# Attention and gated feed-forward on one core: another order of the last stage's block products, later column sums, and w_out prepared at other times

## The chip, the cores and the metric

The kernel runs on one core of a Trainium2 chip. The metric is the device time of one execution in microseconds, lower is better. A core has five engines with queues of their own: TensorE (PE, with its weight loads as PEld), VectorE (DVE), ScalarE (ACT), GpSimd (POOL) and SyncE (SP), which here issues all DMAs. An engine executes its queue in order; an instruction that waits holds up all behind it.

## What is computed

```python
scores = where(causal mask, -1e9, (q @ k^T) / sqrt(64))      # q, k, v: 4 x 12 heads x 448 x 64
attn   = exp(scores - max); attn = attn / (sum(attn) + 1e-9)
x      = (attn @ v), heads side by side                      # 1792 tokens x 768
xn     = x / sqrt(mean(x * x) + 1e-6) * rms_g
g      = xn @ w_gate                                         # 768 x 1536
h      = g / (1 + exp(-g)) * (xn @ w_val)
out    = h @ w_out                                           # 1536 x 768
```

All of it is float32. A matmul operand is split into a rounded part h and the rest l (x = h + l), and a product is three matmuls: h·h, h·l and l·h.

## The kernel before

**Attention and FFN windows.** The tokens are cut into four groups (`GROUPS`) of 512, 512, 512 and 256 columns. Group 0's attention runs first. Then four FFN windows follow, window b for group b, and in each the attention steps of group b + 1 are laid between the FFN's matmuls. A window has 24 units; s counts them from 0 to 95. A unit is 18 matmuls for one 128-column piece of w_gate or w_val (`ffn_part`), in three ticks of six. `AT` says by which third of a unit a window's attention steps are done (of 72): 66, 62, 40. Window 2 (s = 48 to 71) has 30 steps to lay.

**The order is written out by hand.** The program emits instructions in the order of this loop, and each engine executes its own in that order. `post(n, fn)` emits fn n ticks later. `load_w(s + 6)` asks for the weights of a unit eleven ticks after unit s began, `split_w(s + 3)` splits them (ACT casts, POOL or DVE subtracts), and both use a ring of 4 buffers, `wr_p`. A unit's result is stored to `hd` in HBM.

**w_out** comes as 64-bit floats. `load_w64(s + 7)` and `convert(s + 5)` (L381 to L388) turn w_gate, w_val and then w_out's twelve pieces into float32 in HBM (`w32`), one piece per unit, w_out's at s = 19 to 30. Then `wo_sums` (L407 to L426), three times at `SUMS`, builds the sums of w_out's blocks that the last stage needs: loads, four additions 6 ticks later, four stores 12 ticks later. From the fifth unit after the last attention step on, `prep_load` and `prep_split` bring 15 of the 21 pieces of w_out's seven block operands into SBUF and split them (L480, L482), one per unit, in the ring `wr_p`. The last six come at the start of the last stage.

**rms** (L327 to L342) runs once per group. Two matmuls with `ones` sum the squares over the features into bank t; ACT takes the root, DVE four reciprocals. Then four small matmuls put the same sums into columns, again in bank t, and root and reciprocal follow at once. `rcol` scales the rows of the output.

**The last stage** multiplies h by w_out with Strassen-Winograd products: per pair of 128-token blocks seven products (`product`, 18 matmuls of 384 columns, 49 in all for 7 pairs). Products 0 and 1 add up in one PSUM bank, products 5 and 6 in another. `operand(q + 4)`, four products ahead, makes the next stationary operand (ACT cast L512, POOL subtraction L99; for i = 2 four DVE additions first, L504 to L507). `result` takes the sum out of the bank, combines it and stores a block of the output. `load_h` brings a pair's h (1.5 MB) from HBM. PSUM has eight banks: a, t, x, y, m twice, s twice.

Of the kernel before, what the change touches and what calls it, by code (L numbers as in the profile page):

```python
# [14 lines left out]
ALU = mybir.AluOpType  # L15
# [35 lines left out]
HALF = DM // 2  # L51
WARM = [9, 0, 0, 2]
EXTRA = 4
AT = [66, 62, 40, 1]
DP = 3
SUMS = (34, 39, 44)


@with_exitstack
def attention_ffn(ctx: ExitStack, tc: tile.TileContext, qk0, qk1, qk2, v, v2, w, g, out):  # L60
# [19 lines left out]
    ht_p = pool("ht", 6, ffn, side="left")  # L80
    xx_p = pool("xx", 1, ffn, side="left")
    xr_stack = ctx.enter_context(ExitStack())
    xr_p = pool("xr", 6, xr_stack, side="left")
    raw = pool("raw", 4, att, side="right")
    sp_p = pool("sp", 6, att, side="right")
# [226 lines left out]
    def split_x(at):  # L312
        if not waiting:
            return
        b, c = waiting[0]
        if b and c >= 3 and at < (b * NU - 1) * 3 + c // 2:
            return
        waiting.pop(0)
        x, gc = xr[b, c][:, : cols(b)], g_sb[:, c: c + 1]
        h, l = (xx_p.tile([P, W], F32R, tag=f"{n}{c}", name=n, bufs=1 + (c < 3))[:, : cols(b)]  # L320
                for n in ("xh", "xl"))
        nc.scalar.mul(h, x, gc)
        post((T["xl0"] if c < NP - 1 else T["xl"]) if b == 0 else int(c < 3), lambda: nc.vector.scalar_tensor_tensor(  # L323
            out=l, in0=x, scalar=gc, in1=f32(h), op0=ALU.mult, op1=ALU.subtract))
        xh[b, c], xl[b, c] = h, l

    def rms(b, sq):  # L327

        ps = bank("t")[:, : cols(b)]
        nc.tensor.matmul(ps, ones, sq, start=True, stop=True)  # L330
        r = rinv[b] = xx_p.tile([P, W], F32, tag="rms", name="rms", bufs=2)[:, : cols(b)]
        nc.scalar.activation(r, ps, AF.Sqrt, bias=eps, scale=1.0 / DM)
        for i in range(cols(b) // P):
            sl = slice(i * P, (i + 1) * P)
            nc.vector.reciprocal(r[:, sl], r[:, sl])
        n = cols(b) // P
        ps = bank("t")[:, :n]
        for i in range(n):
            nc.tensor.matmul(ps[:, i: i + 1], sq[:, i * P: (i + 1) * P], ones[:, :1], start=True, stop=True)
        rc = rcol[:, W // P * b: W // P * b + n]  # L340
        nc.scalar.activation(rc, ps, AF.Sqrt, bias=eps4, scale=4.0 / DM)
        nc.vector.reciprocal(rc, rc)  # L342

# [86 lines left out]
    def ffn_part(s, ks):  # L432
# [22 lines left out]
        else:  # L455
# [3 lines left out]
                out=hd[b][:, :, f, :], in_=t.rearrange("p (n t) -> p n t", t=2 * P)))  # L459


    ORDER = (("a11", 0), ("a12", 0), ("s2", 0), ("s1", 0), ("s4", 0), ("s3", 0), ("a22", 0))
    WSRC = [lambda m: wo_tile(m, 0), lambda m: wo_tile(m, 1), lambda m: wsum[1][m], lambda m: wsum[0][m],
            lambda m: wo_tile(m + 3, 1), lambda m: wsum[2][m], lambda m: wsum[3][m]]
    wc, side = {}, {}

    def prep_load(j):

        i, m = divmod(j, 3)
        t = wr_p.tile([P, DM], F32, tag="w", name="w_o")  # L470
        nc.sync.dma_start(out=t, in_=WSRC[i](m))
        wt["o", j] = t

# [20 lines left out]
    def operand(q):  # L494

        if q >= 7 * NPAIR:
            return
        p, i = divmod(q, 7)
        t = hp[p]
        a11, a12, a21, a22 = (t[:, 6 * k: 6 * k + 6, P * e: P * e + P] for e in (0, 1) for k in (0, 1))  # L500
        if i == 2:
            s1, s2 = (side["r"].tile([P, 6, P], F32, tag=n, name=n) for n in ("s1", "s2"))
            op["s1"] = s1
            nc.vector.tensor_tensor(s1, a21, a22, op=ALU.add)  # L504
            nc.vector.tensor_tensor(s2, s1, a11, op=ALU.subtract)  # L505
            nc.vector.tensor_tensor(a21, a11, a21, op=ALU.subtract)
            nc.vector.tensor_tensor(a12, a12, s2, op=ALU.subtract)  # L507
            src = s2
        else:
            src = (a11, a12, None, op.get("s1"), a12, a21, a22)[i]  # L510
        h, l = (side["o", q % 4].tile([P, 6, P], F32R, tag=n, name=n) for n in ("oh", "ol"))
        nc.scalar.copy(h, src)  # L512
        pool_op(l, src, ALU.subtract, f32(h))
        op[q] = h, l

    def product(q):
        p, i = divmod(q, 7)
        if i != 1 and i != 6:
            op["ps"] = bank("msssxyy"[i] if i not in (2, 3) else "s", 2 if i in (0, 2, 3) else 1)[:, :HALF]
        ps = op["ps"]  # L520
        (ah, al), (bh, bl) = op.pop(q), wc[i]
        again = i in (1, 6)
        for k in range(6):
            for n, (x, y) in enumerate(((ah, bh), (ah, bl), (al, bh))):
                nc.tensor.matmul(ps, x[:, k, :], y[:, k], start=(k + n == 0 and not again),  # L525
                                 stop=(k == 5 and n == 2), skip_group_check=again)
        return ps

    def result(q, ps):


        p, i = divmod(q, 7)
        r = side["r"]

        def tmp(n):
            op[n] = r.tile([P, HALF], F32, tag=n, name=n)
            return op[n]

        def store(c, e, n):
            nc.sync.dma_start(out=out[P * (2 * p + e): P * (2 * p + e + 1), HALF * n: HALF * (n + 1)], in_=c)  # L540

        def res(u, e, n):
            c = r.tile([P, HALF], F32, tag="c", name="c", bufs=4)
            if u is None:
                nc.scalar.mul(c, ps, rcol[:, 2 * p + e: 2 * p + e + 1])
            else:
                nc.vector.tensor_tensor(c, u, ps, op=ALU.add)  # L547
                nc.scalar.mul(c, c, rcol[:, 2 * p + e: 2 * p + e + 1])  # L548
            store(c, e, n)

        if i == 0:
            nc.scalar.copy(tmp("m1"), ps)  # L552
        elif i == 1:
            res(None, 0, 0)
        elif i == 2:
            u = tmp("u2")
            nc.vector.tensor_tensor(u, op["m1"], ps, op=ALU.add)
        elif i == 3:
            u = tmp("u4")
            nc.vector.tensor_tensor(u, op["u2"], ps, op=ALU.add)  # L560
        elif i == 4:
            res(op["u4"], 0, 1)
        elif i == 5:
            res(op["u4"], 1, 1)
        else:
            res(op["u2"], 1, 0)

# [46 lines left out]
    with tc.manual_schedule():  # L614
# [57 lines left out]
        for s in range(NG * NU):  # L672
            w_ = s // NU
            if s % NU == 0:
                at, goal = done, ends[w_ + 1] + 2 * (w_ == 0) if w_ + 1 < NG else done
            post(T["ld"], lambda s=s: load_w64(s + 7))
            post(T["ld1"], lambda s=s: load_w(s + 6))
            if s in SUMS:
                wo_sums(SUMS.index(s))
            for k0 in (0, 2, 4):  # L680
                ks = [k for k in (k0, k0 + 1) if (s, k) not in early]
                if ks:
                    ffn_part(s, ks)
                i = 3 * (s % NU) + k0 // 2 + 1
                while done < goal and (done - at) < (goal - at) * i / AT[w_]:
                    steps[done]()
                    done += 1
                for _ in range(2):
                    split_x(3 * s + k0 // 2)
                if k0 == 0:  # L690
                    convert(s + 5)
                if k0 == (0 if s < 3 else 4):
                    split_w(s + 3)
                for fn in prep.pop(now[0], []):
                    fn()
                tick()
            if done == len(steps) and att_end is None:
                att_end = s
            if att_end is not None and s == att_end + 5:
                att.close()  # L700
                side["w"] = pool("wc", 1, side="right", reuse_waits="tile")
                for i in range(5):
                    side["w", i] = side["w"]
            if att_end is not None and s >= att_end + 5 and preps < 15:
                prep_load(preps)
                post(2, lambda j=preps: prep_split(j))
                preps += 1
            if s == (NG - 1) * NU + 6:
                assert not waiting
                xr_stack.close()  # L710
                side["h", 0] = side["o", 0] = pool("h0", 1, side="right", reuse_waits="tile")
                load_h(0)
            if s == NG * NU - 4:
                operand(0)
        assert not prep and preps == 15
        while later:
            tick()
        ffn.close()
        side["r"] = side["h", 1] = side["w", 5] = side["w", 6] = pool("r", 1, side="left", reuse_waits="tile")
        ring = pool("ring", 3, side="left", reuse_waits="tile")  # L720
        for i in (1, 2, 3):
            side["o", i] = ring
        operand(1)
        operand(2)
        for j in (15, 16, 17):
            prep_load(j)
        load_h(1)
        operand(3)
        for q in range(7 * NPAIR):
# [6 lines left out]
                        prep_load(j)  # L736
            if q and q % 7 == 0:
                load_h(q // 7 + 1)
            operand(q + 4)
            result(q, ps_)  # L740
            tick()


# [45 lines left out]
```

## Time and profile before

| | us |
|---|---|
| median of 3 runs | 807.07 (806.69 to 812.16) |
| the profiled execution | 806.67 |
| its span, first to last instruction | 804.7 |
| PE busy in the span | 712.0 (88%) |
| DVE, ACT, POOL busy | 448.8, 379.1, 431.8 |

A row of a stage view gives, for a stretch of the span, its length and each engine's busy time with the number of instructions, then the granted TensorE clock (PEclk, 1.00 is 2.4 GHz), the DMA engines' share and GB/s. A row of waits gives who stood idle for whom: us in total, how often, and the longest. A matmul's busy time overlaps the next one's, so the pace is read from starts.

### The profile page before, as it was taken

The page shows a single profiled execution, that of the slowest core. Times are in us where ns is not written, and L with a number is a line of the kernel's source. Part 1 is how long each engine was busy: PE and PEld are TensorE (multiplying, and loading weights), DVE is VectorE, ACT ScalarE, POOL GpSimd, SP SyncE. Part 2 cuts the span into 40 slices and gives each one's busy share as a digit, 9 for nine tenths or more (in the row PEclk, how much of TensorE's full clock was granted, in tenths as well). Part 3 has the DMA queues.
Part 4 walks back from the last instruction along what each step waited for, and adds up shares of the span by engine and source line. Part 5 has one row for each costly group of instructions (what it writes and reads, how often), then busy time and mean ns, then how long its engine had stood idle before and what let it go on. Part 6 is the DMA issues. An engine that isn't in the chain of part 4 may idle for free. (4 is left out here: it accounts for less than half of the span.)

```text
span 804.7 us, 12298 instructions
## 1 busy us (share of the span) xinstructions
PE 712.0 (88%) x4302; PEld 583.7 (73%) x4302; DVE 448.8 (56%) x893; ACT 379.1 (47%) x824; POOL 431.8 (54%) x343
## 2 busy tenths in 40 slices
PE   8788799997978999997999989985968888978977
PEld 6555567775756777766778778875967877978977
DVE  5866768887789956573756432475564133033131
ACT  7867778685454544443535132454443223222321
POOL 5985344485338668553653634554458345445441
PEclk9998899999899999998999999998989889989989
DMA  8653858787587685875857414688642312321201
GB/s 271 224 180 112 268 192 265 257 278 277 189 301 253 243 289 203 307 272 180 271 175 208 146 60 150 210 264 267 209 164 73 108 38 89 109 82 56 99 30 39
DMA packets 61708, 149.04 MB, mean 185 GB/s; under 512 B 7056, under 2 KB 27536, under 8 KB 60752
## 3 DMA queue, kind: packets, MB, share of 16 engines
q1 hardware_dynamic: 61648, 148.27, 55.1%
q8 instruction: 34, 0.56, 0.3%
q14 instruction: 26, 0.21, 0.1%
HBM read 112.86 MB, written 35.39 MB: 184 GB/s over the span
## 5 line engine op out<-in xcount | busy, mean ns | idle before, releaser
L442 PE MATMUL m_ps<-xh,w_h 128*128 128x512 f32 (+1 forms) x570 | 225.2, 395 | 7.1 <-DVE gr L450 6.5
L444 PE MATMUL m_ps<-xh,w_l 128*128 128x512 f32 (+1 forms) x570 | 212.9, 374 | 5.5 <-POOL w_l L99 5.5
L443 PE MATMUL m_ps<-xl,w_h 128*128 128x512 f32 (+1 forms) x570 | 212.0, 372 | 0.1
L99 POOL TENSOR_TENSOR w_l<-w_r,w_h 128x768 fp32r<-128x768 f32 x60 | 112.8, 1890 | 62.4 <-ACT w_h L396 61.5
L207 POOL TENSOR_SCALAR sp<-sp,rs 128x384 f32<-128x384 f32 (+3 forms) x132 | 86.5, 672 | 91.1 <-DVE rs L211 89.8
L442 PEld LDWEIGHTS m_ps<-xh,w_h 128*128 128x128 f32 x570 | 111.4, 195 | 25.9 <-ACT woh L480 6.8
L444 PEld LDWEIGHTS m_ps<-xh,w_l 128*128 128x128 f32 x570 | 110.8, 194 | 25.6 <-POOL w_l L99 6.7
L443 PEld LDWEIGHTS m_ps<-xl,w_h 128*128 128x128 f32 x570 | 111.4, 195 | 13.6 <-DVE xl L323 0.4
L202 ACT ACTIVATE sp<-sp,nm 128x128 f32<-128x128 f32 (+3 forms) x168 | 87.1, 521 | 60.4 <-DVE nm L199 60.4
L99 POOL TENSOR_TENSOR ol<-h_r,oh 128x768 fp32r<-128x768 f32 x35 | 68.9, 1971 | 53.3 <-ACT oh L512 53.3
L451 ACT ACTIVATE t_sb<-gr 128x512 f32<-128x512 f32 (+1 forms) x48 | 27.7, 577 | 130.4 <-DVE gr L450 130.4
L273 PEld LDWEIGHTS a_ps<-pt,v_r 128*64 128x64 f32 (+1 forms) x864 | 40.8, 138 | 44.7 <-ACT pt L253 13.4
L273 PE MATMUL a_ps<-pt,v_r 128*64 128x128 f32 (+2 forms) x864 | 58.5, 269 | 16.5 <-ACT pt L253 8.0
L396 ACT CAST w_h<-w_r 128x768 fp32r<-128x768 f32 x72 | 58.7, 825 | 23.9 <-DMA w_r<-w 20.0
L382 POOL TENSOR_SCALAR w<-w 128x768 f32<-128x768 f32 x36 | 44.3, 1230 | 38.6 <-ACT w_c L381 27.6
L512 ACT CAST oh<-h_r 128x768 fp32r<-128x768 f32 x35 | 29.2, 835 | 72.1 <-PE m_ps L525 31.2
L199 DVE CUSTOM_DVE_ANT_0 sp<-s_ps,mask 128x128 f32<-128x128 f32 (+3 forms) x136 | 49.8, 414 | 19.5 <-PE s_ps L190 17.9
L247 PE MATMUL t_ps<-ident,sp 128*128 128x128 f32 (+1 forms) x309 | 51.8, 280 | 7.3 <-DVE pt L251 6.0
L251 DVE COPY pt<-t_ps 128x384 f32<-128x384 f32 (+1 forms) x71 | 42.3, 596 | 27.4 <-PE t_ps L247 27.4
L247 PEld LDWEIGHTS t_ps<-ident,sp 128*128 128x128 f32 (+1 forms) x309 | 38.2, 140 | 23.3 <-DVE pt L251 6.0
L99 POOL TENSOR_TENSOR ol<-s,oh 128x768 fp32r<-128x768 f32 x14 | 30.4, 2177 | 45.7 <-ACT oh L512 45.7
L525 PE MATMUL y_ps<-woh,oh 128*128 128x384 f32 x84 | 34.4, 410 | 23.0 <-DVE c L547 23.0
(112 smaller groups left out, 1335.8 us busy)
## 6 DMA issues: line engine op xcount, KB each, us to landing
w<-in_w SPq DMA_DIRECT2D x36, 768.0 KB, 5.7
w_r<-w SPq DMA_DIRECT2D x72, 384.0 KB, 4.4
qk_r<-in_qk SPq DMA_DIRECT2D x48, 256.0 KB, 4.3
h_r<-hd SPq DMA_DIRECT2D x7, 1536.0 KB, 6.7
w<-w_c SPq DMA_DIRECT2D x24, 384.0 KB, 2.8
hd<-t_sb SPq DMA_DIRECT2D x36, 256.0 KB, 3.8
qk_r<-in_qk SPq DMA_DIRECT2D x12, 512.0 KB, 4.4
v_r<-in_v SPq DMA_DIRECT2D x12, 448.0 KB, 8.2
```

The source lines that it names most:

```text
L99: nc.gpsimd.tensor_tensor(out_, a, b, op=op)
L199: nc.vector.tensor_tensor_reduce(out=sp, in0=ps, in1=mk, scale=nsc, scalar=3.0e38, op0=ALU.add, op1=ALU.min, accum_out=nm)
L202: post(T["exp" if p >= ENDS[0] else "exp0"], lambda: nc.scalar.activation(sp, sp, AF.Exp, bias=nm, scale=-1.0, accum_out=sm))
L207: pr["norms"].append(lambda: nc.gpsimd.tensor_scalar(sp, sp, rs, 1.0, op0=ALU.mult, op1=ALU.mult))
L247: nc.tensor.transpose(ps[:kb, at: at + P], pr["sp"][e][:, o + kb * j: o + kb * (j + 1)], ident)
L251: nc.vector.tensor_copy(pt[:kb, :at], ps[:kb, :at])
L273: nc.tensor.matmul(av_ps[e * D: (e + 1) * D, p % 2, q0: q0 + n], raw_v[p][:kb, h, j, e, :], pr["pt", e][:kb, a0: a0 + n], start=(j == 0), ...
L382: (T["c1"], lambda: nc.gpsimd.tensor_scalar(hf_, hf_, 0.0, 1.0, op0=ALU.mult, op1=ALU.mult)),
L396: nc.scalar.copy(h, t)
L442: nc.tensor.matmul(ps, wh[:, k, :], mh, start=(first and k == ks[0]), stop=False)
L443: nc.tensor.matmul(ps, wh[:, k, :], ml, start=False, stop=False)
L444: nc.tensor.matmul(ps, wl[:, k, :], mh, start=False, stop=(last and k == 5))
```

## The change

In the last stage the seven products of a pair run in another order. Before, their banks were m m s s x y y, where the second m and the second y add to the bank of the product just before. After, they are m s m s y x y. The operands, w_out's pieces (`WSRC`) and the results follow that order; the additions of the long operand stand at i = 1 (three of them) and i = 5 (the fourth). `result(q)` is emitted ahead of `operand(q + 4)`. Operand 1 is made before the stage begins, with s1, s2 and the first operands' buffers in the pool h0; operands have two pools of 2 buffers each, and `c` has 3 in place of 4.

In `rms` the small matmuls move 8 ticks later and into bank x, and DVE copies their sums; one root and one reciprocal for all groups stand at the head of the last stage, ahead of `load_h(1)` and operand 3.

w_out's pieces are loaded from s = 22 and converted from s = 26 on, one per two units. `wo_sums` runs at s = 50, 54 and 58. Window 1 lays its attention steps up to third 64 and window 2 up to third 54. From the second unit after the last attention step, two pieces per unit are loaded and split, out of a pool of 2 buffers of their own. The first three chunks of x's parts for even groups come from a pool `xa`, which is given back earlier.

```diff
-AT = [66, 62, 40, 1]
+AT = [66, 64, 54, 1]
-SUMS = (34, 39, 44)
+SUMS = (50, 54, 58)
+LATE = 22
...
@@ rms
-        n = cols(b) // P
-        ps = bank("t")[:, :n]
-        for i in range(n):
-            nc.tensor.matmul(ps[:, i: i + 1], sq[:, i * P: (i + 1) * P], ones[:, :1], start=True, stop=True)
-        rc = rcol[:, W // P * b: W // P * b + n]
-        nc.scalar.activation(rc, ps, AF.Sqrt, bias=eps4, scale=4.0 / DM)
-        nc.vector.reciprocal(rc, rc)
+
+        def columns():
+            n = cols(b) // P
+            ps = bank("x")[:, :n]
+            for i in range(n):
+                nc.tensor.matmul(ps[:, i: i + 1], sq[:, i * P: (i + 1) * P], ones[:, :1], start=True, stop=True)
+            rc = rcol[:, W // P * b: W // P * b + n]
+            nc.vector.tensor_copy(rc, ps)
+
+        post(8, columns)
...
@@ prep_load
-        t = wr_p.tile([P, DM], F32, tag="w", name="w_o")
+        t = side["w"].tile([P, DM], F32, tag="w", name="w_o", bufs=2) if j < 15 else \
+            wr_p.tile([P, DM], F32, tag="w", name="w_o")
...
@@ operand
-        if i == 2:
-            s1, s2 = (side["r"].tile([P, 6, P], F32, tag=n, name=n) for n in ("s1", "s2"))
-            op["s1"] = s1
+        if i == 1:
+            s1, s2 = (side["s"].tile([P, 6, P], F32, tag=n, name=n) for n in ("s1", "s2"))
+            op["s1"], op["s2"] = s1, s2
             nc.vector.tensor_tensor(s1, a21, a22, op=ALU.add)
             nc.vector.tensor_tensor(s2, s1, a11, op=ALU.subtract)
             nc.vector.tensor_tensor(a21, a11, a21, op=ALU.subtract)
-            nc.vector.tensor_tensor(a12, a12, s2, op=ALU.subtract)
-            src = s2
-        else:
-            src = (a11, a12, None, op.get("s1"), a12, a21, a22)[i]
-        h, l = (side["o", q % 4].tile([P, 6, P], F32R, tag=n, name=n) for n in ("oh", "ol"))
+        if i == 5:
+            nc.vector.tensor_tensor(a12, a12, op["s2"], op=ALU.subtract)
+        src = (a11, op.get("s2"), a12, op.get("s1"), a21, a12, a22)[i]
+        h, l = (side["o", q % 4].tile([P, 6, P], F32R, tag=n, name=n, bufs=2) for n in ("oh", "ol"))
...
@@ product
-        if i != 1 and i != 6:
-            op["ps"] = bank("msssxyy"[i] if i not in (2, 3) else "s", 2 if i in (0, 2, 3) else 1)[:, :HALF]
-        ps = op["ps"]
+        n = "msmsyxy"[i]
+        if i not in (2, 6):
+            op["bank", n] = bank(n, 2 if n in "ms" else 1)[:, :HALF]
+        ps = op["bank", n]
...
@@ the loop over units
-            post(T["ld"], lambda s=s: load_w64(s + 7))
+            c = s + 7 if s + 7 < NU else NU + (s - LATE) // 2 if s >= LATE and (s - LATE) % 2 == 0 else NC
+            post(T["ld"], lambda c=c: load_w64(c))
...
-                    convert(s + 5)
+                    convert(s + 5 if s + 5 < NU else NU + (s - LATE - 4) // 2
+                            if s >= LATE + 4 and (s - LATE) % 2 == 0 else NC)
...
-            if att_end is not None and s >= att_end + 5 and preps < 15:
-                prep_load(preps)
-                post(2, lambda j=preps: prep_split(j))
-                preps += 1
+            if att_end is not None and s >= att_end + 2:
+                for j in range(preps, min(preps + 2, 15)):
+                    prep_load(j)
+                    post(2, lambda j=j: prep_split(j))
+                    preps += 1
...
             if s == NG * NU - 4:
                 operand(0)
+            if s == NG * NU - 2:
+                operand(1)
...
@@ the last stage
-        operand(1)
         operand(2)
         for j in (15, 16, 17):
             prep_load(j)
+        nc.scalar.activation(rcol, rcol, AF.Sqrt, bias=eps4, scale=4.0 / DM)
+        nc.vector.reciprocal(rcol, rcol)
         load_h(1)
         operand(3)
         for q in range(7 * NPAIR):
...
+            result(q, ps_)
             operand(q + 4)
-            result(q, ps_)
             tick()
```

## Rows read from the trace of the kernel before

**Rows 1.** Stages: length; PE, PEld, DVE, ACT, POOL busy; PEclk; DMA; GB/s.
```profile
420.00:480.00 60.00, 57.84 (x517) 45.38 (x516) 28.03 (x64) 23.13 (x49) 26.64 (x24) 0.99 0.46 141
480.00:593.10 113.10, 100.45 (x618) 90.74 (x617) 54.05 (x73) 46.94 (x69) 54.17 (x29) 0.96 0.60 198
593.10:804.70 211.60, 171.62 (x885) 167.02 (x883) 63.44 (x67) 61.90 (x89) 102.79 (x51) 0.90 0.23 83
```
**Rows 2.** The chain that ended last: start us, us, what.
```profile
630.92 3.02 PE m_ps L525 x17
...
638.70 6.25 PE s_ps L525 x36
...
649.56 2.48 DVE s L505
...
653.77 0.48 DVE c L547
654.39 5.96 PE y_ps L525 x18
660.35 2.98 PE m_ps L525 x17
...
797.25 3.42 PE y_ps L525 x18
```
**Rows 3.** Timeline of the last stage's start: start us, us, instruction, [idle before <-releaser].
```profile
593.23 0.33 PE L525 MATMUL m_ps<-woh,oh 128*128 128x384 f32 x1
...
601.85 0.47 ACT L552 COPY m<-m_ps 128x384 f32<-128x384 f32 x1
...
605.53 0.83 ACT L480 CAST woh<-w_o 128x768 fp32r<-128x768 f32 x1 [3.22 <-DMA w_o<-wsum]
```
**Rows 4.** Waits of TensorE over the run: us in total, times, longest.
```profile
PE y_ps L525 <- DVE c L547: 23.0, 7, 6.4
PE m_ps L525 <- ACT m L552: 12.9, 7, 5.8
PE t_ps L339 <- ACT rms L332: 11.2, 4, 4.6
...
PE m_ps L442 <- DVE gr L450: 6.5, 2, 5.3
PE t_ps L247 <- DVE pt L251: 6.0, 5, 3.2
PE m_ps L444 <- POOL w_l L99: 5.5, 5, 1.6
```
**Rows 5.** Stages again, around one pause of the last stage.
```profile
629.32:653.21 23.89, 20.75 (x117) 20.10 (x116) 6.74 (x8) 7.74 (x11) 11.68 (x7) 1.00 0.25 91
653.21:660.04 6.83, 5.65 (x18) 5.68 (x19) 1.03 (x2) 0.61 (x1) 2.25 (x1) 0.50 0.08 29
683.93:687.34 3.41, 3.41 (x12) 3.41 (x12) 0.00 (x0) 0.35 (x1) 0.91 (x1) 0.50 0.16 58
```
**Rows 6.** Groups of instructions from 602 on: busy us, mean ns; idle before.
```profile
L99 POOL TENSOR_TENSOR ol<-h_r,oh 128x768 fp32r<-128x768 f32 x33 | 65.2, 1979 | 47.7 <-ACT oh L512 47.7
...
L512 ACT CAST oh<-h_r 128x768 fp32r<-128x768 f32 x32 | 26.7, 835 | 69.7 <-PE m_ps L525 31.2 <-PE s_ps L525 24.7 <-PE x_ps L525 13.8
```
**Rows 7.** DMA issues on the page: count, KB each, median us to landing.
```profile
h_r<-hd SPq DMA_DIRECT2D x7, 1536.0 KB, 6.7
```
**Rows 8.** Stages again, behind the second `rms`.
```profile
199.24:206.07 6.83, 6.42 (x21) 5.45 (x22) 6.44 (x8) 1.34 (x3) 1.82 (x1) 0.50 0.00 1
```
**Rows 9.** Splits and units: w_o landing, POOL's split, `gr` per two units.
```profile
DMA to landing us min/median/max: 3.2/3.9/8.7
...
L99 POOL TENSOR_TENSOR wol<-w_o,woh 128x768 fp32r<-128x768 f32 x8 | 16.2, 2027 | 18.9 <-ACT woh L480 18.9
...
L450 DVE TENSOR_TENSOR gr<-m_ps,rms x5: 690/692/692, 486.8 to 519.5; 128x512 f32<-128x512 f32 x5
...
L450 DVE TENSOR_TENSOR gr<-m_ps,rms x7: 409/424/425, 562.7 to 589.4; 128x256 f32<-128x256 f32 x7
```

More of the change, by code (lines that the diff above doesn't have):

```diff
@@ L82, in attention_ffn @@
     xr_stack = ctx.enter_context(ExitStack())
+    xa_p = pool("xa", 1, xr_stack, side="left")
     xr_p = pool("xr", 6, xr_stack, side="left")
@@ L319, in split_x @@
         x, gc = xr[b, c][:, : cols(b)], g_sb[:, c: c + 1]
-        h, l = (xx_p.tile([P, W], F32R, tag=f"{n}{c}", name=n, bufs=1 + (c < 3))[:, : cols(b)]
+        h, l = ((xa_p if c < 3 and b % 2 == 0 else xx_p).tile([P, W], F32R, tag=f"{n}{c}", name=n)[:, : cols(b)]
                 for n in ("xh", "xl"))
@@ L459, in ffn_part @@
                 out=hd[b][:, :, f, :], in_=t.rearrange("p (n t) -> p n t", t=2 * P)))
-    ORDER = (("a11", 0), ("a12", 0), ("s2", 0), ("s1", 0), ("s4", 0), ("s3", 0), ("a22", 0))
-    WSRC = [lambda m: wo_tile(m, 0), lambda m: wo_tile(m, 1), lambda m: wsum[1][m], lambda m: wsum[0][m],
-            lambda m: wo_tile(m + 3, 1), lambda m: wsum[2][m], lambda m: wsum[3][m]]
+    WSRC = [lambda m: wo_tile(m, 0), lambda m: wsum[1][m], lambda m: wo_tile(m, 1), lambda m: wsum[0][m],
+            lambda m: wsum[2][m], lambda m: wo_tile(m + 3, 1), lambda m: wsum[3][m]]
     wc, side = {}, {}
@@ L517, in product @@
         p, i = divmod(q, 7)
-        if i != 1 and i != 6:
-            op["ps"] = bank("msssxyy"[i] if i not in (2, 3) else "s", 2 if i in (0, 2, 3) else 1)[:, :HALF]
-        ps = op["ps"]
+        n = "msmsyxy"[i]
+        if i not in (2, 6):
+            op["bank", n] = bank(n, 2 if n in "ms" else 1)[:, :HALF]
+        ps = op["bank", n]
         (ah, al), (bh, bl) = op.pop(q), wc[i]
-        again = i in (1, 6)
+        again = i in (2, 6)
         for k in range(6):
@@ L542, in res @@
         def res(u, e, n):
-            c = r.tile([P, HALF], F32, tag="c", name="c", bufs=4)
+            c = r.tile([P, HALF], F32, tag="c", name="c", bufs=3)
             if u is None:
@@ L553, in result @@
         elif i == 1:
+            nc.vector.tensor_tensor(tmp("u2"), op["m1"], ps, op=ALU.add)
+        elif i == 2:
             res(None, 0, 0)
-        elif i == 2:
-            u = tmp("u2")
-            nc.vector.tensor_tensor(u, op["m1"], ps, op=ALU.add)
         elif i == 3:
-            u = tmp("u4")
-            nc.vector.tensor_tensor(u, op["u2"], ps, op=ALU.add)
+            nc.vector.tensor_tensor(tmp("u4"), op["u2"], ps, op=ALU.add)
         elif i == 4:
+            res(op["u4"], 1, 1)
+        elif i == 5:
             res(op["u4"], 0, 1)
-        elif i == 5:
-            res(op["u4"], 1, 1)
         else:
@@ L698, in attention_ffn @@
                 att_end = s
-            if att_end is not None and s == att_end + 5:
+            if att_end is not None and s == att_end + 2:
                 att.close()
@@ L710, in attention_ffn @@
                 xr_stack.close()
-                side["h", 0] = side["o", 0] = pool("h0", 1, side="right", reuse_waits="tile")
+                side["h", 0] = side["o", 0] = side["o", 1] = side["s"] = pool("h0", 1, side="right", reuse_waits="tile")
                 load_h(0)
@@ L719, in attention_ffn @@
         side["r"] = side["h", 1] = side["w", 5] = side["w", 6] = pool("r", 1, side="left", reuse_waits="tile")
-        ring = pool("ring", 3, side="left", reuse_waits="tile")
-        for i in (1, 2, 3):
+        ring = pool("ring", 2, side="left", reuse_waits="tile")
+        for i in (2, 3):
             side["o", i] = ring
-        operand(1)
         operand(2)
```

## Prediction

> **What bounds the kernel now.** I read the stages first [rows 1]. In the last one, 593.1 to 804.7 us, no other engine is busy for half of the time, TensorE is, and its granted clock is only 0.90. So TensorE there is both waiting and slow. The chain of waits says why [rows 2]. Two products in a row take 6.25 us for 36 matmuls, 3.13 us each. From the first product (593.23 [rows 3]) to the end of the last (797.25 + 3.42 = 800.67) the 49 products take 207.4 us; 49 × 3.13 is 153.4. So 54.0 us of this stage is not work. It has three causes.
>
> First, inside a pair (about 29.4 us, 630.92 to 660.35, against 7 × 3.13 = 21.9) the second y product must wait until VectorE has read the first one's sum, and VectorE does that read (653.77) after four additions of `operand`. The second m product likewise waits for ScalarE's copy, which stands behind a cast. Over the run these waits are 23.0 and 12.9 us [rows 4]. Second, each such pause is followed by a stretch at half clock [rows 5]: 1.00 (2.4 GHz) for 23.9 us up to the pause, then 0.50, the 1.2 GHz level, for 6.83 us; the y product in it takes 5.96 us instead of 3.13 [rows 2]. Third, the first pair takes 37.7 us (593.23 to 630.92).
>
> Before 593 the waits of TensorE [rows 4] name three smaller places: 11.2 us in `rms` (L339, for the square root that reads bank t), 6.0 us of transposes behind VectorE, and 6.5 + 5.5 us of FFN matmuls behind the weight splits.
>
> **The last stage.** The order of banks becomes m s m s y x y. A product that adds to a bank now has another product, 3.13 us, between it and its predecessor. What must fit under it: for m, the copy (0.47 us [rows 3]) behind no cast of the same step, since `result` now comes before `operand`; for y, one addition of 0.5 us [rows 2]. Both fit, so I cost the 23.0 + 12.9 us as gone apart from the first pair.
>
> Is something else late next? `operand(q + 4)` is issued after product q, so it has three products, 9.4 us, before it is needed. A plain operand needs a cast of 0.83 and a POOL subtraction of 1.98 [rows 6], 2.8 us. The long one (i = 1) needs s1 and s2, at 2.48 each as s2 has it now [rows 2], behind one addition of 0.5, then cast and subtraction: 8.3 us. It fits, by 1.1 us. Per pair POOL needs 7 × 1.98 = 13.9 us of 21.9 and VectorE less. h_r is asked for at the head of a pair, lands 6.7 us later [rows 7] and is used after four products, 12.5 us. `c` with 3 buffers: a buffer comes back after at least 12 us of products, while one store is 192 KB. So six of the seven pairs at 21.9: 131.4 us.
>
> First pair. Operands 0 and 1 now stand ready before the stage. But the three casts of w_out pieces (j = 15 to 17) still stand ahead of the copy of m on ScalarE; that copy came at 601.85, 8.6 us after the start [rows 3]. The product that needs it is now the third, due 6.3 us after the start, so some 2.8 us of pause (9.1 before), and half a clock stretch, 1.7 to 3.4 us. The next three casts come after their loads (605.53 and later [rows 3]) and hold up the casts of operands 5 and 6 by some 3 us. The sum is 8 us over 21.9; bounds 2 (all hidden) and 15.8 (as now). Stage: 131.4 + 21.9 + 8 = 161.3, a gain of 46.1 us (38 to 52).
>
> Do the many changes of bank cost clock? Four products in a row in four banks (s, s, x, y, from 638.70 on [rows 2]) ran without a wait inside the stretch at 1.00 [rows 5]. The Trainium skill, page "TensorE: Matmul & The Clock Gate", section "A second HAM failure mode: psum-queue depth-cycling", tells of a kernel that cycled through PSUM banks at each iteration and whose clock kept switching between its levels. By the row the stage gains 46.1 us, by that rule some 18 less (rival A). I take the row; no such switching without a pause shows in this trace.
>
> **Column sums.** `rms` no longer waits for the root before the small matmuls: they go to bank x, 8 ticks later. Of 11.2 us [rows 4] the first of the four cases stays, since transposes into t follow it at once; in the second a transpose follows after six matmuls, so a little may stay: gain 9. The pause was followed by half clock ([rows 8] is one of three such stretches, 6.83, 6.83 and 3.41 us long; half of each is lost, 8.5 together). I take 6 of it. Unknown: the wait for bank x; the nearest row, VectorE's read of a bank at 0.5 us [rows 2], bounds it at 2 us over the four. Net 15 (8 to 20). The four roots become one at the head of the last stage; its table load sits in front of operand 3's cast, within the 8 us above.
>
> **Conversions of w_out.** Twelve of them move from one per unit (s = 19 to 30) to one per two units (26 to 48). Each is VectorE work, two shifts, and in that part of the run VectorE is what the transposes waited for: most of the 6.0 us [rows 4]. I take 4 (0 to 8, with a half-clock stretch that follows one of them). The same work lands where TensorE hardly waits now. The sums move to s = 50, 54, 58, four units apart: their store (12 ticks) now falls just ahead of the next sums' loads into the same tiles, so SP stands until it has landed, with q, k, v and weight loads behind it. Weight loads run about three units ahead, so I charge 2 us (0 to 8). Spreading attention (AT 54 instead of 40) moves matmuls between units; I cost that at nothing: TensorE is busy for 57.8 of 60 us there as it is (420 to 480 [rows 1]).
>
> **Splits of w_out.** The last attention step moves from s = 60 to 65 (30·i/54 > 29 gives i = 53). So 15 pieces go two per unit over s = 67 to 74, from a pool of their own with 2 buffers. Each load must wait until the piece two before has been split: landing 3.9 and POOL 2.03 [rows 9] with a cast of 0.83 [rows 6] make 6.8 us per unit. A unit takes 4.1 us in the third window (486.8 to 519.5 over 8 units) and 2.2 in the fourth [rows 9]. SP holds these loads in line with the FFN's weight loads, so the weights become late: 7 × 6.8 = 47.6 us of loads against 4 × 4.1 + 3 × 2.2 = 23.0 of matmuls, less some 8 us of lead (three units of 4.1 less a landing of 3.9), a stall of 17, and 4 behind h_r (6.7 [rows 7] less a unit of 2.2): 21 us. Before, one piece per unit ran to s = 79 in a pool shared with the weights, and cost 6.5 + 5.5 us of waits [rows 4] and some 3.4 of clock (0.96 over 113 us [rows 1] is 4.5, a part of it from the stretch before): 15.4. Loss 5; bounds +12 (weights with four buffers of their own never wait) and -18 (each stall with a half-clock stretch).
>
> **Sum.** 46 + 15 + 4 - 2 - 5 = 58. The span of 804.7 becomes 746.7; the profiled execution took 806.67, 1.97 more, so 748.6; it lies 0.4 under the median of the runs, 807.07. I say 748.5.
>
> **Rivals.**
> A. The clock does not hold in the last stage: every pair keeps the half-clock stretches of now (6.83 and 3.41 us in turn [rows 5], 2.6 us lost a pair), with no wait left. For it: each pair now has one. Against: each follows a pause of over a microsecond that the change takes out. 7 × 2.6 = 18 us: 767. It is the rule of the Trainium skill cited above (page "TensorE: Matmul & The Clock Gate", same section). Chance 0.07.
> B. The split pool is worse than costed: ScalarE stands at a cast whose load is late, tanh and weight casts behind it, and TensorE drops to half clock between. The bound of -18 and 8 us lost at the sums: 768. For it: the 6.8 against 2.2 us. Against: the same chain ran before with half the pieces per unit. Chance 0.10.
> C. The reordering does not free the products: the long operand's chain, at 8.3 us plus queueing, is late once per pair by 2 us with a clock stretch of 1.7 to 3.4 behind it. 7 × 4.5 = 31: 780. Against: the POOL subtraction before it is done 3 us earlier, so VectorE runs s1 and s2 alone. Chance 0.06.
> D. Slower. At the splits the gain of 58 is lost if an iteration costs (58 + 17 + 23 + 8) / 7 = 15.1 us instead of 6.8, as each 1 us more costs 7. The longest landing seen there, 8.7 [rows 9], in every iteration gives 11.6, or 782; from 15.1 on it decides, and at 16.3 the time is 815. Chance 0.02.
> E. Better: the splits gain 6 instead of losing 5, the first pair costs 4 instead of 8, the conversions give 8, and all clock after `rms` comes back: 748.5 - 11 - 4 - 4 - 2.5 = 727. Chance 0.12.
> The forecast itself, 735 to 762, has 0.63.
>
> **Range.** It leaves out D, C and the far halves of E and B, 0.19 in all: 730 to 769. Faster by over 1% (about what a measurement of this kernel can tell from no change) holds all cases but D and the far end of C: 0.94; same 0.04; slower 0.02.
>
> **What would show it.** Right: in the last stage pairs of 21.9 us, granted clock near 1.00 after the first pair, no wait of y for `c` or of m for `m` beyond the first pair; L339 without a wait on the root; the transposes' wait on VectorE shorter. Splits: loads of w_o in twos, 6 to 7 us apart, and FFN units of 5 to 7 us at s = 72 to 77. Wrong: pairs over 23 us with a wait on `ol` or `oh` (C), half clock without a pause (A), or SP standing at `w_o` for over 8 us a time (B, D).

## The result

After: 748.74 us (median of 4 runs, 746.04 to 750.16) against 807.10 before (4 runs, 806.69 to 812.16): a ratio of 0.926, 95% interval 0.921 to 0.931. The profiled execution took 747.44 us, its span is 745.6.

The stage view of after (columns as in [rows 1]; the last stage begins at 578.4):

```profile
480.00:578.40 98.40, 83.86 (x533) 77.91 (x532) 47.16 (x69) 41.75 (x61) 44.13 (x24) 0.90 0.62 206
578.40:745.60 167.20, 157.76 (x884) 156.51 (x883) 51.90 (x67) 63.65 (x91) 96.23 (x51) 0.98 0.29 105
...
502.30:550.70 48.40, 35.43 (x217) 33.48 (x216) 23.34 (x33) 21.89 (x34) 20.52 (x12) 0.79 0.72 240
...
602.90:609.80 6.90, 6.05 (x19) 6.05 (x20) 2.54 (x3) 1.42 (x3) 6.87 (x4) 0.51 0.08 29
609.80:741.20 131.40, 131.40 (x754) 131.40 (x753) 34.40 (x51) 47.56 (x69) 71.70 (x39) 1.00 0.27 97
```

From 609.8 on TensorE is busy all of the time at clock 1.00; before, this stage stood at 0.90. What is left of trouble lies in two places: the units s = 72 to 84 (502.3 to 550.7, clock 0.79) and the first pair, with its one stretch at half clock from 602.9. The chain that ended last, against [rows 2]:

```profile
609.24 3.46 PE m_ps L530 x18
612.70 3.14 PE s_ps L530 x18
...
622.09 3.12 PE y_ps L530 x18
625.21 3.18 PE x_ps L530 x18
628.39 3.18 PE y_ps L530 x18
631.57 3.18 PE m_ps L530 x18
...
738.40 3.19 PE y_ps L530 x18
```

From 609.24 on every product follows the last without a gap, the second y (628.39) too. TensorE's waits over the run, against [rows 4]:

```profile
PE m_ps L447 <- DVE gr L455: 5.7, 2, 3.6
PE x_ps L249 <- DVE rcol L345: 4.2, 1, 4.2
...
PE t_ps L249 <- DVE pt L253: 3.4, 4, 1.6
PE x_ps L343 <- DVE nm L201: 3.3, 1, 3.3
PE m_ps L449 <- POOL w_l L101: 3.0, 4, 1.6
...
PE m_ps L530 <- ACT m L557: 2.4, 1, 2.4
PE y_ps L530 <- POOL ol L101: 2.0, 1, 2.0
...
PE y_ps L530 <- POOL wol L101: 1.0, 1, 1.0
PE t_ps L249 <- ACT rms L334: 1.0, 2, 0.8
```

The 23.0 us of y behind `c` are gone, of the 12.9 of m 2.4 are left, of the 11.2 in `rms` 1.0. New are two waits around the column sums in bank x, 4.2 and 3.3; the first of them, as r9 below shows, stands where another wait stood before.

Where the time went, stage by stage, in the profiled executions. A column is one kernel, a row the time from the first matmul of unit s to that of the next unit named, in us; r3, r14, r5, r6 and r13 are runs below.

| | before | r3 | r14 | after | r5 | r6 | r13 |
|---|---|---|---|---|---|---|---|
| s = 3 to 24 | 127.5 | 123.0 | 118.4 | 118.6 | 124.7 | 118.3 | 118.7 |
| 24 to 48 | 175.0 | 174.0 | 165.3 | 159.8 | 169.8 | 159.4 | 159.1 |
| 48 to 72 | 133.5 | 133.3 | 132.4 | 137.5 | 131.5 | 137.5 | 135.3 |
| 72 to 84 | 42.1 | 42.8 | 41.5 | 48.4 | 48.0 | 41.2 | 38.0 |
| 84 to the first product | 27.7 | 27.8 | 28.1 | 27.8 | 27.7 | 27.7 | 28.0 |
| last stage | 207.4 | 204.0 | 206.6 | 163.1 | 160.1 | 160.5 | 157.0 |

Of the 59 us, 44.3 come from the last stage, 24.1 from the first two windows, and 10.3 are lost between s = 48 and 84.

### The profile page after: what moved, and what is told of

Its sections match the earlier page's. It is cut to its first block, busy times and chain, and to the rows that moved or that the text cites. A ratio compares the mean times of both kernels' runs of the same rounds, so it can differ in the third digit from the quotient of the medians.

```text
span 745.6 us, 12274 instructions
## 1 busy us (share of the span) xinstructions
PE 693.1 (93%) x4302; PEld 571.5 (77%) x4302; DVE 438.5 (59%) x894; ACT 379.6 (51%) x822; POOL 425.8 (57%) x343
## 5 line engine op out<-in xcount | busy, mean ns | idle before, releaser
L101 POOL TENSOR_TENSOR w_l<-w_r,w_h 128x768 fp32r<-128x768 f32 x60 | 115.1, 1925 | 75.6 <-ACT w_h L401 72.3
L456 ACT ACTIVATE t_sb<-gr 128x512 f32<-128x512 f32 (+1 forms) x48 | 27.7, 577 | 129.9 <-DVE gr L455 129.8
L101 POOL TENSOR_TENSOR ol<-h_r,oh 128x768 fp32r<-128x768 f32 x35 | 65.8, 1882 | 32.1 <-ACT oh L516 29.0
L389 DVE SCALAR_TENSOR_TENSOR w<-w 128x768 int32<-128x768 int32 x36 | 50.1, 1393 | 7.2 <-POOL w L387 7.1
L457 DVE SCALAR_TENSOR_TENSOR t_sb<-t_sb,gr 128x512 f32<-128x512 f32 (+1 forms) x48 | 35.5, 741 | 23.0 <-ACT t_sb L456 22.1
L455 DVE TENSOR_TENSOR gr<-m_ps,rms 128x512 f32<-128x512 f32 (+1 forms) x47 | 29.1, 620 | 30.9 <-PE m_ps L449 30.7
```

The lines of the kernel that those rows point to most:

```text
L101: nc.gpsimd.tensor_tensor(out_, a, b, op=op)
L389: (T["c2" if c >= 5 else "c20"], lambda: nc.vector.scalar_tensor_tensor(out=lo, in0=lo, scalar=29, in1=hi, op0=ALU.logical_shift_right, op ...
```

## The experiments

Before had medians of 804.6 to 805.6 in them (7 to 11 runs each). A difference to after is read from the two ratios; its interval is about 5 us either way, so stages are set beside it.

**The order of the products alone (r1).** Before, with `WSRC`, `operand`, `product` and `result` as after; `operand` still ahead of `result`, operand 1 still made in the stage.

```diff
-            op["ps"] = bank("msssxyy"[i] ...
+        n = "msmsyxy"[i]
```

> The kernel before with the new order of products alone; operand q + 4 still comes ahead of result q, and operand 1 (now the long one) is made after the FFN. Theory: the order alone is not enough. The m product is freed (one cast of 0.83 us and the copy of 0.47 fit under 3.13 us), but VectorE's read of the first y still stands behind the long operand's three additions (0.95 + 2.48 + 1 to 2.5 us), so y waits 2 to 3 us once per pair and a half-clock stretch follows: pairs of 26 to 27 us, time 792 to 800. Rival: a product between the two is all that is needed, pairs of 22 us, time 766 as in the next run.

Measured: 763.48 us, 0.948 (0.945 to 0.951). My theory fell: the wait does not come back. The last stage takes 163.1 us, pairs 22.0. The timeline of r1 around the first y product of a pair (start us, us, instruction, [idle before <- releaser]):

```profile
662.37 0.34 PE L525 MATMUL y_ps<-woh,oh 128*128 128x384 f32 x1
...
663.04 0.95 DVE L504 TENSOR_TENSOR s<-h_r 128x768 f32<-128x768 f32 x1
...
663.36 2.34 POOL L99 TENSOR_TENSOR ol<-h_r,oh 128x768 fp32r<-128x768 f32 x1 [1.28 <-ACT oh L511]
...
664.03 2.49 DVE L505 TENSOR_TENSOR s<-s,h_r 128x768 f32<-128x768 f32 x1
...
666.44 0.95 DVE L506 TENSOR_TENSOR h_r<-h_r 128x768 f32<-128x768 f32 x1
...
667.31 0.54 DVE L547 TENSOR_TENSOR c<-u,y_ps 128x384 f32<-128x384 f32 x1
...
668.61 0.34 PE L525 MATMUL y_ps<-woh,oh 128*128 128x384 f32 x1
```

The three additions need nothing of the y product, so they start right behind the result before it and run beside it. The sum is read at 667.31, 2.0 us after the product's last matmul began (665.32). Before, the next product was the other y and waited; now the x product stands between, and y comes at 668.61 with 0.8 us to spare (667.31 + 0.54 = 667.85). The edit also takes the fourth addition from this place, but the three that are left still make the read end 2.2 us after the product's last matmul (665.66), so a y that came next would have waited. The product in between is what frees the pair.

**The order, and `result` first (r2).** r1 and the swap in the loop:

```diff
+            result(q, ps_)
             operand(q + 4)
-            result(q, ps_)
```

> The same with result q ahead of operand q + 4. Theory: pairs of 21.9 us at a granted clock near 1.00 but for the first pair, which loses some 13 us as the long operand 1 and the w_out casts come after the FFN: 807 - 54 + 13 = 766 (760 to 772). Rival, the clock does not hold when the bank changes with each product: half-clock stretches in every pair, 2.6 us each, 784.

Measured: 761.08 us, 0.945 (0.943 to 0.947), inside r1's interval. Pairs 22.0, last stage 161.6. `result` ahead of `operand` brings nothing that these runs can tell.

**The column sums alone (r3).** Before, with the new `columns` in `rms` and the one root.

> The kernel before with the change in rms alone: small matmuls 8 ticks later in bank x, one root at the end. Theory: 10 of the 11.2 us of waits go and most of the half-clock stretches behind them, but VectorE's copy out of x and its reads of x now make TensorE wait 3 to 4 us in two of four places: net gain 8 to 11 us, 796 to 799. Rival: nothing is given back at x, gain 15, 792; or all is given back, 805 or more.

Measured: 799.29 us, 0.993 (0.991 to 0.995), a gain of 6. The table has it nearly all in s = 3 to 24; from 24 to 48 there is almost none, and the timeline of r3 behind the second `rms`, VectorE's queue, shows why:

```profile
211.44 0.95 DVE L387 SCALAR_TENSOR_TENSOR w<-w 128x768 int32<-128x768 int32 x1
...
216.55 0.95 DVE L389 SCALAR_TENSOR_TENSOR wo_c<-wo_c,w 128x768 int32<-128x768 int32 x1
...
218.01 2.82 DVE L323 SCALAR_TENSOR_TENSOR xl<-xr,g_sb,xh 128x512 fp32r<-128x512 f32 x2
220.75 0.15 DVE L343 COPY rcol<-x_ps 128x4 f32<-128x4 f32 x1
...
220.96 1.00 PE L190 MATMUL x_ps<-qk_r 64*128 64x384 f32 x1 [7.53 <-DVE rcol L343]
```

The sums are in bank x at 211; their copy, 0.15 us of work, stands behind the conversion of w_out (`w`, `wo_c`) and splits of x, for which VectorE itself stood 3.30 us until ScalarE's `xh`, and TensorE waits 7.53 us for the bank. So of the 11.2 us in `rms` 8.1 go (3.1 are left in r3) and 7.5 come; the gain that remains lies in the clock, with 23.9 us at half clock ahead of s = 72 in place of 34.1.

**Column sums and conversions together (r14).** r3, and w_out loaded and converted in every second unit from s = 22 on with the sums at 50, 54, 58.

> The kernel before with two parts of the change: the column sums late, and w_out's conversions in every second iteration from s = 22 on, with the sums at s = 50, 54 and 58. Old order of products, old splits. Theory: the two add up, 6 for the column sums and 7 for the conversions: 790 to 794. Rival: they help each other, since a column sum waits for whatever stands ahead of rcol's copy on VectorE, and the conversions stand there at the second rms: 780 to 786.

Measured: 785.41 us, 0.978 (0.974 to 0.981), 18 us less than before and 12 to 14 less than r3. The rival held: they help each other. The wait of 7.5 us at the second `rms` is not in r14.

**Conversions back (r5).** After, with

```diff
-            c = s + 7 if s + 7 < NU else NU + (s - LATE) // 2 if s >= LATE and (s - LATE) % 2 == 0 else NC
+            c = s + 7
```

and `convert(s + 5)`. The conversions then stand at s = 19 to 30; the 43 in the expectation is a slip.

> The changed kernel with the conversions of w_out back at their old place: one in every iteration from s = 43 on, inside the second window, not every second one from s = 22 on; the column sums stay late, and the rest stays too. Theory: the spreading of the conversions is worth much more than the 4 us that I gave it, for in the changed kernel the stages up to s = 48 are 25 us shorter, and the column sums alone brought 6: 12 to 18 us back, 761 to 767. Rival, as predicted: 4 us, so about 753, and the 25 us come from the sums having left the windows while the conversions in them cost little. Second rival: no loss at all, 749.

Measured: 755.89 us, 0.939 (0.935 to 0.943): 10 us by the ratios, 7 by the medians. That lies between the theory's 12 to 18 and the rival's 4: the first two windows lose 16 us (table), but the third gives 6.0 of them back. In after only the last of the twelve conversions and the tail of the one before fall into the third window, so it is hardly their own work that is saved there. The column sums' wait for bank x is 0.6 us in place of 3.3, and the half clock behind it in after (0.50 for 3.41 us from 374.31) does not come. What ties these two to the conversions is not shown. And r3's wait for the copy is there again; TensorE's waits in r5:

```profile
PE x_ps L192 <- DVE rcol L345: 6.6, 1, 6.6
...
PE x_ps L343 <- DVE nm L201: 0.6, 1, 0.6
```

**Column sums back (r12).** After, with `rms` as before.

> The changed kernel with the column sums back in rms, in bank t with root and reciprocal at once; all else stays. Theory: they are worth 6 us, as they were when made alone: 754 to 756. Rival: alone they were worth so little because rcol's copy stood behind the conversions of w_out (a wait of 7.5 us at 213), which the changed kernel has moved away; then they are worth the 15 us that I predicted: 761 to 765.

Measured: 750.09 us, 0.933 (0.930 to 0.936): 5 us by the ratios, 1 by the medians. The theory's side, if anything less; the 15 are refuted. With the column sums in bank t again, the wait for the root is 5.3 us in TensorE's waits in r12, not the 11.2 of before:

```profile
PE t_ps L341 <- ACT rms L334: 5.3, 4, 2.2
```

**The old splits (r6).** After, with one piece per unit in `wr_p` from the fifth unit on and `AT` 40.

> The changed kernel with the splits of w_out as before: one piece per unit, in the ring of the weights, and the fourth group's attention done by third 40 of 72 instead of 54. Theory: two pieces per unit through two buffers cost what the trace shows, 48.5 us from s = 72 to 84 against 42.1, so that undoing them brings 5 to 7 us: 742 to 744. Rival: the stall is paid either way, for the h_r load and the weight loads share the queue in both, and the time stays: 747 to 750.

Measured: 740.84 us, 0.920 (0.917 to 0.923): 5 us by the ratios, 8 by the medians. Units 72 to 84 take 41.2 us again; the stage view of r6 has them at clock 0.92:

```profile
502.30:543.50 41.20, 30.57 (x218) 28.66 (x217) 26.67 (x32) 20.66 (x31) 19.48 (x12) 0.92 0.78 262
```

**Two rings for the pieces (r4).** After, with every second piece in `wr_p`, so that the load of a piece need not wait for the split of the one two before.

```diff
-        t = side["w"].tile([P, DM], F32, tag="w", name="w_o", bufs=2) if j < 15 else \
+        t = side["w"].tile([P, DM], F32, tag="w", name="w_o", bufs=2) if j < 15 and j % 2 else \
```

> The changed kernel, but the even ones of the first 15 w_out pieces are loaded into the ring of the FFN weights (4 buffers), the odd ones into the pool of 2: a buffer is reused after two units in place of one. Theory: the 6 us from load to split set the pace of the units at the window's change, so with twice the distance the loss there (22.6 us over s = 72 to 83) shrinks by 6 to 12 us: 737 to 743. Rival: the loads' rate or ScalarE's order sets that pace and not the buffers: within 3 us of the changed kernel, 746 to 751.

Measured: 740.16 us, 0.920 (0.917 to 0.923). In the stage view of r4 units 72 to 84 take 39.2 us at clock 0.96 instead of 48.4 at 0.79:

```profile
505.10:544.30 39.20, 29.32 (x218) 27.82 (x217) 28.04 (x31) 18.81 (x29) 21.91 (x11) 0.96 0.76 249
```

So pieces two by two are no loss in themselves; two buffers for them are.

**Splits earlier (r7).** After, with `AT` 40 in place of 54, pairs and two buffers kept. The splits then begin at s = 62 in place of 67; the expectation says 76 by mistake.

> The changed kernel with the fourth group's attention window begun at s = 62 instead of 76, so that the fifteen pieces of w_out, still two by two into two buffers, are split in units of that window which TensorE fills mostly itself, and end sooner. Theory: the 13.0 us idle and 20.5 us at half clock between s = 72 and 84 come from the pairs' 6.1 us against units of 4.1 us; with more units ahead of the last ones, most of the waiting goes: 736 to 742. Rival: the attention of the fourth group, now packed into fewer units, pays it back in its own waits, 746 to 752.

Measured: 746.74 us, 0.928 (0.924 to 0.932): the rival's time, but not its reason. Units 72 to 84 fall to 35.1 us, and s = 48 to 60, into which the attention is packed, rise from 80.2 to 87.9. But r6, with the same `AT`, has 87.6 there and gets it back in s = 60 to 72, 49.9 us instead of 57.2. In r7 these units take 57.9, for the splits stand in them now: units 68 to 71 take 6.0 us on average, 4.1 in after. So the price of two buffers moved with the splits and was paid at another place.

**Column sums in another bank (r9).** After, with group 0's column sums in bank m and group 2's one tick behind their sums.

```diff
-            ps = bank("x")[:, :n]
+            ps = (bank("x") if b else bank("m", 2))[:, :n]
-        post(8, columns)
+        post(1 if b == 2 else 8, columns)
```

> The changed kernel with the column sums of the first third in bank m instead of x, and those of the last third posted one tick behind their sums instead of eight. Theory: the two waits that I held to 2 us, 4.2 us for the copy of rcol ahead of the x transposes and 3.3 us for bank x ahead of the columns, and the half clock behind the second (3.4 us lost at most by it), go: 740 to 744. Rival: at the first place TensorE is held by ScalarE's copy of pt anyway, and the late addition only moves, so that at most 3 us come back: 746 to 749.

Measured: 745.27 us, 0.926 (0.922 to 0.929): not to be told from after, so the theory is not borne out. At the first place the 4.2 us for `rcol` became two waits of 2.63 and 1.86 us for ScalarE's `pt`, which was as late; TensorE's waits in r9 (3.9 in after):

```profile
PE a_ps L275 <- ACT pt L255: 8.3, 8, 2.6
```

The kernel before waits for the same two copies at the same place, 4.6 us; its timeline:

```profile
83.46 1.11 PE L273 MATMUL a_ps<-pt,v_r 128*64 128x256 f32 x2 [3.16 <-ACT pt L253]
...
85.97 1.54 PE L273 MATMUL a_ps<-pt,v_r 128*64 128x256 f32 x6 [1.40 <-ACT pt L253]
```

So the 4.2 us in after are no loss against before: the wait for `rcol` covers one that was there already. At the second place the 3.3 us are gone and s = 48 to 72 is 2.0 us shorter, though a stretch of 3.41 us at half clock still comes (384.28).

**The first pair (r10).** After, with pieces 15 to 20 loaded at s = 94, `result` ahead of `prep_split`.

> The changed kernel with the first pair of the last stage mended: pieces 15 to 20 of w_out are loaded one iteration before the stage, in buffers that are free then, and the result of a product is made before the next split is issued. Theory: the first pair's 30.6 us are 22 of products and 8.6 of waits on m, wol and ol and of the half clock behind them; loads in time take 5 to 7 of these away: 742 to 744. Rival: the wait is for POOL's long operand itself (it is 2.0 us late with its loads in time too): 747 to 749.

Measured: 742.00 us, 0.921 (0.917 to 0.925). First pair 24.7 us instead of 30.6; the wait for `m` is gone, and so is the half clock; the 2.0 for POOL's `ol` stays. The theory held; the rival's wait is the smaller part.

**The three mendings together (r13).** r4, r9 and r10.

> The changed kernel with the three mendings together: w_out's pieces split in turns in the ring of the weights and in the pool of two, the first column sums in bank m and the last ones a tick behind their sums, and pieces 15 to 20 loaded an iteration before the last stage. Theory: 8.6 and 3.5 and 6.7 us add up: 728 to 733. Rival: the first pair's mending and the rings draw on the same loads, and one of the two gains is lost: 735 to 738.

Measured: 730.05 us, 0.908 (0.906 to 0.911), the fastest of all: 19 us less than after by the medians, 14 by the ratios, for 18.8 forecast. They add up within the intervals (table: 72 to 84 38.0, last stage 157.0).

## Why the prediction was right

748.5 forecast, 748.74 measured. The mechanism of the largest term held. That the total meets to 0.3 us is luck: two of the smaller terms were wrong, in opposite directions, and a third came out by another make-up than told.

**The last stage** was costed at 161.3 us and took 163.1: pairs of 21.9 forecast, 22.0 measured (the second 22.4, as it begins in the half clock), the first 29.9 and 30.6. The order did it: r1 has 42 of the 59 us. Of the first pair's terms the later casts (waits of 1.0 for `wol` and 2.0 for `ol`, 3 forecast) and the half clock (6.83 us from 603.0, so 3.4 lost, 1.7 to 3.4 forecast) came as told. So did the pause for the copy of m, 2.4 us for 2.8, behind the casts of pieces; the timeline of ScalarE in after:

```profile
583.38 0.84 ACT L485 CAST woh<-w_o 128x768 fp32r<-128x768 f32 x1 [0.88 <-DMA w_o<-w]
585.04 1.77 ACT L485 CAST woh<-w_o 128x768 fp32r<-128x768 f32 x2 [0.82 <-DMA w_o<-w]
586.72 0.47 ACT L557 COPY m<-m_ps 128x384 f32<-128x384 f32 x1
```

The reason given for y, one addition of 0.5 us under a product, holds in after, but `result` first was not needed for it (r1, r2).

**Clock.** Rival A is refuted: from 609.8 to 741.2, six pairs that change bank at each product, the granted clock is 1.00; so it is in r1 and r2. The Trainium skill, "TensorE: Matmul & The Clock Gate", section "A second HAM failure mode: psum-queue depth-cycling", speaks of pauses between groups of matmuls when banks are cycled; here there are none, and the clock does not switch. The pauses were the cause before, not the changes of bank.

**Column sums: 15 forecast, 6 alone (r3), 1 to 5 when undone (r12).** The step that failed is the wait for bank x, bounded at 2 us from the duration of a read, 0.5; the sum then left even these 2 out, for 9 + 6 - 2 is 13. The copy is shorter still, 0.15, but what counts is VectorE's queue: 7.53 us ahead of the copy in r3 (the 4.3 at the first `rms` only cover the wait for `pt`, see r9), and 3.3 in after, where the sums wait for bank x behind `nm`. I named what is queued behind a waiting instruction, and not what stands ahead of the one that frees the bank.

**Conversions: 4 forecast, 12 to 14 when added to r3 (r14), 7 to 10 when undone (r5).** The step that failed is "VectorE work, two shifts". A conversion begins with a ScalarE step (L381) and goes on with one on POOL, and the ScalarE step stood ahead of the root in the second `rms` of before. Its timeline there:

```profile
194.85 0.82 ACT L396 CAST w_h<-w_c 128x768 fp32r<-128x768 f32 x1
...
196.70 0.90 ACT L381 ACTIVATE wo_c<-w 128x768 f32<-128x768 f32 x1 [1.03 <-DMA w<-wo_c]
197.61 1.28 ACT L332 ACT_TABLE_LOAD   x1
...
198.91 0.69 ACT L332 ACTIVATE rms<-t_ps,eps 128x512 f32<-128x512 f32 x1
...
199.65 1.65 PE L339 MATMUL t_ps<-ones,acc 128*128 128x1 f32 x7 [3.66 <-ACT rms L332]
```

Of the 3.66 us that I read as a price of the place of the column sums, 1.93 are L381 (0.90) with its wait (1.03) for the store of an earlier piece, which frees the buffer `wo_c`. So a part of the 11.2 us belonged to the conversions, which r12 confirms with 5.3. The two terms together were forecast at 19 and measured at 18 (r14): I had the lost time of that stretch about right and put it under the wrong edit.

**Splits: -5 forecast, about -5 to -8 measured (r6).** The mechanism is as told; w_o's loads are asked for in twos 6 us apart (6.8 forecast, as they landed in a median of 3.1 us, not 3.9), with a weight load behind each two; SP's timeline in after:

```profile
489.20 0.33 SPq L476 DMA_DIRECT2D w_o<-w  x1
491.80 0.32 SPq L476 DMA_DIRECT2D w_o<-wsum  x1
492.17 0.42 SPq L371 DMA_DIRECT2D w_r<-w  x1
496.06 2.17 SPq L476 DMA_DIRECT2D w_o<-wsum  x2
498.28 0.43 SPq L371 DMA_DIRECT2D w_r<-w  x1
501.95 1.85 SPq L476 DMA_DIRECT2D w_o<-w  x2
```

Units 72 to 77 took 5.2 us on average, inside the 5 to 7 named, but singly 7.9, 3.8, 2.3, 7.1, 5.2 and 4.6. The size is partly luck. At 2.2 us each, units 72 to 84 would take 26.4; after is 22.0 above that and before 15.7, where the prediction had 21 and 15.4. But it counted the 21 as waiting alone, and after has 13.0 us idle (48.40 - 35.43) and up to 10.2 lost at half clock (0.79 over 48.4). Rivals B and D did not come: no step at `w_o` took SP over 3.4 us.

**The sum of the runs.** Order with `result` first 44 (r2), sums and conversions 18 (r14), splits -5 to -8 (r6): 54 to 57 of 59. The rest is within the intervals. What stays open: s = 24 to 48 takes 165.3 us in r14 and 159.8 in after; the other place of attention (`AT` 64) and the pool `xa` fall there and were not tried alone. The traces say only where it lies: at the end of that stretch TensorE waits 4.9 us for VectorE's `t_sb` in r14, with 6.83 us at half clock from 361.06, and 1.7 us with no half clock in after. Not tried alone either were the moved `wo_sums`, costed at -2, which are part of r14.

## What to carry to other kernels

Put independent work between two accumulations into one bank, not a faster read: one product in between made it unimportant here whether VectorE's read or three additions came first (r1, r2). Cost a small step on a shared engine by what stands ahead of it in that queue where it will be emitted, not by its duration. Before you book a wait on one edit, list every engine that the neighbouring edit's work also runs on; and when you give loads their own buffers, count how many loads must be in flight, since two here held the queue with the weights in it.

## What the hardware showed

An addition on VectorE and a subtraction on POOL over the same 128x768 float32 shape hold each other up. In r1's rows above L504, under way when the POOL subtraction of 663.36 begins, keeps its 0.95 us, and the subtraction takes 2.34 instead of 1.85. L505 begins while the subtraction runs and takes 2.49; L506, after it, takes 0.95 again. L505 ends 0.8 us after the subtraction does (666.52 against 665.70), about its own 0.95. So the one that came second seems to have stood still rather than run slower; that is a reading of the times, no run tests it. In after, where POOL stands idle beside the additions, all three take 0.95; its timeline:

```profile
669.80 0.95 DVE L509 TENSOR_TENSOR s<-h_r 128x768 f32<-128x768 f32 x1
...
670.79 0.96 DVE L510 TENSOR_TENSOR s<-s,h_r 128x768 f32<-128x768 f32 x1
671.66 0.95 DVE L511 TENSOR_TENSOR h_r<-h_r 128x768 f32<-128x768 f32 x1
...
672.77 1.85 POOL L101 TENSOR_TENSOR ol<-s,oh 128x768 fp32r<-128x768 f32 x1 [3.94 <-ACT oh L516]
```

So the 2.48 us [rows 2] that the prediction took for each of s1 and s2 is the price of that meeting, and the long operand's chain takes 4.8 us here (669.80 to 674.62), not the 8.3 of rival C. The Trainium skill, "SBUF — State Buffer", section "Who interferes with whom", states that a VectorE instruction with two SBUF inputs contends with a GpSimd instruction that reads SBUF; the traces agree.
